# Splitting a unit's row maxima on GpSimd before they are transposed, in a fused attention and Fourier kernel

## The chip, the cores and the metric

The kernel runs on one core of one Trainium2 chip. The metric is the device time of one execution in microseconds; less is better. Times "before" are those of the kernel as it stood ahead of the change.

## The reference

Two sublayers read the same input, and a gate mixes them. Cut to what is computed:

```python
x = A_x                                           # (1, 2048, 640) float32
g = sigmoid((x * gate_w).sum(-1, keepdims=True))
# attention, 32 heads of width 20
qkv = (x @ wqkv).reshape(B, S, 3, 32, 20)         # q, k, v
p = softmax(q @ k.T * 20 ** -0.5)                 # per head, 2048 x 2048
a = (p @ v).reshape(B, S, 640) @ wo
# Fourier mixing of the same x
u, w = x @ dft_hid_re.T, x @ dft_hid_im.T
b = dft_seq_re @ u - dft_seq_im @ w
return g * a + (1 - g) * b
```

The weights wqkv and wo are drawn small and then multiplied by 64. The softmax subtracts each row's maximum.

## The kernel before

Most products are made from two rounded parts of each fp32 value (`split`: a rounded copy, then the rest as a second rounded value), by three matmuls (`three`). `R` is the rounded type (`float32r`), `F32` is plain fp32.

**Units.** The 32 heads are taken in 16 pairs; a pair's queries come in two halves of 1024. One pair with one half is a unit, so there are 32 units (`NU`). The stacks `qst` and `kst` hold, for each of the pair's two heads, 60 rows of split queries and keys in one half of the partitions (0 to 59 and 64 to 123). Behind them come two more rows: in `kst` ones, in `qst` the negated row maximum of each query, as a rounded part and its rest. So the second score matmul gives logits with the maximum subtracted already, and the exponential can follow at once.

**Two score passes.** In the first pass (`s_mm`, line 170) a step computes two 128 x 512 blocks of scores, and VectorE takes the maximum over 512 keys (`mx`, line 172). A unit has 32 such steps. When the last one is done, `max_nm` reduces the four partial maxima of each query and negates them (`nm`, 128 x 16, line 186), and `max_chain` transposes them on TensorE (line 204), splits the result on VectorE (lines 114 and 115 by way of `split`), and sends the rows into `qst` by four transfers on the SyncE queue (lines 212 and 213). In the second pass (line 873) scores are computed again, transposed and with the maximum in them; ScalarE takes the exponential (line 875). The av matmuls (line 532) multiply it by the values, with a column of ones for the sums. At a unit's end `unit_end` divides by the sums, which takes a way over DRAM and one multiplication on GpSimd (line 562).

**The order of work.** It is written out by hand. A head phase loads and projects; the last projections (`qk_tile`, lines 118 to 120) are mixed with `HEAD` segments. A segment is one tile of the Fourier transform along the hidden axis (line 362) with four steps of the first pass, and one comes with every third projection tile. Then comes the main loop of 256 cycles. A cycle follows the string `ORDER`: eight matmuls of the second pass ("e", four steps), eight of the first pass ("m"), filling matmuls ("F"), and at its end a burst ("B") with the av matmuls of two key blocks. The first pass is `LEAD` steps ahead of the second, so the last `LEAD` steps of the loop have no "m". The fillings are, in this order: the other tiles of the hidden transform (one for each cycle), 56 tiles of the transform along the sequence (three cycles each, `dft_step`, line 613), and 30 half rows of the output projection (line 684; one cycle each, the last `SLOW` ones two cycles).

**GpSimd and the transfers.** The transform along the sequence is made by seven products of sums of blocks (`PRODUCTS`). GpSimd adds the loaded blocks and splits them: cosine blocks into `part` (`load_c`: lines 493, 114, 115), two for each tile, made ahead through a ring of three buffers; and the other operand into `x` (`load_a`: lines 507, 114, 115) for the product that follows. It also adds finished tiles to earlier ones (`yt`, line 711). ScalarE and VectorE read a finished tile first (`m`, lines 632 and 633). Each engine takes its instructions in the order in which the program gives them out. `at_step(i, fn)` gives out a piece of work when the second pass comes to step i.

In `burst`, units whose maxima have just ended stand in the list `ends`: `max_nm` is given out first, `max_chain` after the av matmuls of the same burst.

Of the kernel before, what the change touches and what calls it, by code (L numbers as in the profile page):

```python
# [10 lines left out]
F32 = mybir.dt.float32  # L11
R = mybir.dt.float32r
AF = mybir.ActivationFunctionType
ALU = mybir.AluOpType
AX = mybir.AxisListType
# [3 lines left out]
P = 128  # L19
# [10 lines left out]
NU = 2 * NP  # L30
# [6 lines left out]
FIRST = {"e": (0, 0, 1, 1), "m": (1, 1, 1, 1)}  # L37


LEAD = 41  # L40


FILL = {4: (0, 8, 7, 0)}
HEAD = 10

# [12 lines left out]

LONG = (0, 0, 0, 0, 0, 0, 0)
FULL = 1
SLOW = 4
PRE = range(FULL, NS)
UNITS = len(PRODUCTS) * HT

# [3 lines left out]
def f32(ap):  # L70
    return ap.bitcast(F32)
# [3 lines left out]
def mix_kernel(ctx: ExitStack, tc: tile.TileContext, xa, wqk, wb, cdft, wo, out):  # L75
    nc = tc.nc
    pe, act, dve, pool, sp = nc.tensor, nc.scalar, nc.vector, nc.gpsimd, nc.sync
    ctx.enter_context(tc.manual_schedule())

    def pools(**kw):  # L80
        return ctx.enter_context(tc.tile_pool(**kw))

    const = pools(name="const", bufs=1)
    small = pools(name="small", bufs=1)
# [13 lines left out]

    ident = const.tile([P, P], F32, name="ident")
    make_identity(nc, ident)  # L100
    kst = [const.tile([P, S], R, name=f"kst{i}") for i in range(2)]
    qst = [const.tile([P, S], R, name=f"qst{i}") for i in range(2)]
    for t in kst:
# [6 lines left out]
    def split(dst1, dst2, src, e1, e2):  # L110
        if e1 is act:
            act.activation(dst1, src, AF.Copy)  # L112
        else:
            e1.tensor_copy(dst1, src)  # L114
        e2.tensor_tensor(dst2, src, f32(dst1), op=ALU.subtract)  # L115
# [8 lines left out]
    def bank():  # L124
        return ps_w.tile([P, 512], F32, name=f"ps{next(turn) % 5}")
# [23 lines left out]
    def q_unit(n):  # L149
        u = n % 2 * (S // 2)  # L150
        return qst[n // 2 % 2][:, u : u + S // 2]

    mx, nms, ends = {}, {}, []
    now, later = [-1], {}

    def at_step(i, fn):
        later.setdefault(i, []).append(fn)
# [16 lines left out]
    def s_end(i):  # L174
        n, s = divmod(i, 32)
        if n < NU and s == 31:
            if now[0] < 0:
                max_nm(n)
            else:
                ends.append(n)  # L180
        if s == 1 and 0 < n <= NU and now[0] < 0:
            max_chain(n - 1)

    def max_nm(n):
        nms[n] = small.tile([P, 16], F32, name="nm", bufs=2)
        dve.tensor_reduce(nms[n], mx.pop(n).rearrange("p h q c -> p (h q) c"), axis=AX.X, op=ALU.max, negate=True)

    def s_step(i):
        for fn in [s_mm(i, h) for h in range(2)]:
# [10 lines left out]

    def max_chain(n):
        q = q_unit(n)
        pt = bank()[:16, :P]
        pe.transpose(pt, nms.pop(n), ident)
        m1 = small.tile([16, P], R, name="m1")
        m2 = small.tile([16, P], R, name="m2")
        split(m1, m2, pt, dve, dve)

        def rows():
            for h in range(2):  # L210
                b = 64 * h + KROWS
                sp.dma_start(f32(q[b : b + 1, :]), f32(m1[8 * h : 8 * h + 8, :]))
                sp.dma_start(f32(q[b + 1 : b + 2, :]), f32(m2[8 * h : 8 * h + 8, :]))

        if now[0] < 0:
            rows()
        else:
            at_step(now[0] + 2, rows)
# [49 lines left out]
    def load_wqk(c):  # L268
        raw = raw_tile()[:, : ND * P].rearrange("p (d c) -> p d c", d=ND)
        sp.dma_start(raw, wqk[c])  # L270

        def finish():
            w = part_tile().rearrange("p z c -> p (z c)")[:, : 2 * ND * P].rearrange("p (z d c) -> p z d c", z=2, d=ND)
            split(w[:, 0], w[:, 1], raw, act, dve)
            wt[c] = w

        return finish
# [19 lines left out]
    def flush(keep=0):  # L297
        while len(stores) > keep:
            sp.dma_start(*stores.pop(0))
# [52 lines left out]
    def hid_tile(i, read_out):  # L352
        j, st = divmod(i, NS)
        hf, ri = divmod(j, 2)
        new_y(0), new_y(1)
        w = wt["b", 2 + j]
        t, cs = st // 4, slice(st % 4 * P, (st % 4 + 1) * P)
        for d in range(ND):
            for z, (xz, wz) in enumerate(((0, 0), (0, 1), (1, 0))):
                for h in range(2):  # L360
                    r = slice(64 * h, 64 * h + 64)
                    pe.matmul(yp[h][:, :HE], xs[xz][t][r, d, cs], w[r, wz, d, :HE],  # L362
                              start=d == 0 and z == 0, stop=d == ND - 1 and z == 2)
                if (d, z) != (ND - 1, 2):
                    yield
        a = raw_tile()[:, :HE]
        y0, y1 = yp[0][:, :HE], yp[1][:, :HE]

        def read():
            act.activation(a, y0, AF.Copy, scale=-1.0 if ri else 1.0)  # L370
            dve.tensor_tensor(a, a, y1, op=ALU.subtract if ri else ALU.add)  # L371

        read_out(read, (a_scr[ri, hf, st], a))
        yield


    def segment(i, steps):
        def read_out(read, args):
            read()
            stores.append(args)  # L380

        tile_ = hid_tile(i, read_out)
        for n in FILL[steps]:
            run_s(step + 1)
            for _ in range(n):
                next(tile_)
# [3 lines left out]
    def run_s(upto):  # L390
        nonlocal step
        while step < upto:
            s_step(step)
            step += 1
# [42 lines left out]
    for n, c in enumerate(order):  # L437
        for t in range(4):
            m = 4 * n + t
            if m % 3 == 0 and hid_done < HEAD:  # L440
                segment(hid_done, 4)
# [4 lines left out]
            if t == 1:  # L446
                if n + 1 < len(order):
                    fin()
                if n + 2 < len(order):
                    fin = load_wqk(order[n + 2])  # L450
    run_s(LEAD)
    flush()
# [219 lines left out]
    def out_tile(tt, hf):  # L672
        new_y(0), new_y(1)
        if hf == 0:
            k = tt - PRE[0]
            yo[tt] = f32(a_tile(1, 12 + k) if k < 4 else a_tile(0, k)).rearrange("p z c -> p (z c)")
            assert all(st[tt, h] == 0 for h in range(2))
            sp.dma_start(yo[tt], y_scr[tt])
        o = opre[tt]
        for d in range(ND - 1):  # L680
            for z, (oz, wz) in enumerate(((0, 0), (0, 1), (1, 0))):
                for h in range(2):
                    r = slice(64 * h, 64 * h + 64)
                    pe.matmul(yp[h][:, :HE], o[r, oz, d], wos[d, hf][r, wz], start=d == 0 and z == 0, stop=d == ND - 2 and z == 2)  # L684
                if (d, z) != (ND - 2, 2):
                    yield
        m = apool[0].tile([P, HE], F32, name="m", bufs=2)
        y0, y1 = yp[0][:, :HE], yp[1][:, :HE]
        g = gate[:, tt : tt + 1]

        def read():
            if now[0] < total - LEAD:
                act.activation(m, y0, AF.Copy, scale=g)
            else:
                dve.tensor_scalar(m, y0, g, 1.0, op0=ALU.mult, op1=ALU.mult)
            dve.scalar_tensor_tensor(m, y1, g, m, op0=ALU.mult, op1=ALU.add)

        def add():
            y = yo[tt][:, hf * HE : (hf + 1) * HE]
            pool.tensor_scalar(y, y, ngate[:, tt : tt + 1], float(signs[tt, hf]), op0=ALU.mult, op1=ALU.mult)  # L700
            pool.tensor_tensor(y, y, m, op=ALU.add)

        extras.append((now[0], read))
        extras.append((now[0] + 3, add))
        yield
# [35 lines left out]
    def start_dft():  # L741
        flush()
        wide.release()
        apool.append(pools(name="apool", bufs=1))
        make_sel()
# [25 lines left out]
    def read_later(read, args):  # L771
        extras.append((now[0], read))
        at_step(now[0] + 2, functools.partial(sp.dma_start, *args))

    HID = 4 * NS - HEAD
    fills = itertools.chain(*(hid_tile(HEAD + g, read_later) for g in range(HID)), itertools.chain.from_iterable(dft_step(g) for g in range(NS * UNITS)),
                            itertools.chain.from_iterable(out_tile(tt, hf) for tt in PRE for hf in range(2)))
# [3 lines left out]
    start = 4 * HID  # L781
# [10 lines left out]
    for u in range(2 * len(PRE)):  # L792
        n = 2 if u >= 2 * len(PRE) - SLOW else 1
        cycles.append((at_tile, at_tile + n, 3 * (ND - 1)))
# [42 lines left out]
    def end(i):  # L837
        if i % 4 == 2:
            c = i // 4
            if c + HEAD in (NS, 2 * NS):  # L840
                at_step(i + 2, load_wb(3 + (c + HEAD) // NS, pool, pool))
            if c in (HID - 18, HID - 17, HID - 16):
# [9 lines left out]

    heads = {"e": 0, "m": 2 * LEAD}

    def score(kind):
        x = heads[kind]
        heads[kind] += 1
        i, z = divmod(x, 2)
        h = z ^ FIRST[kind][(i - (LEAD if kind == "m" else 0) - 1) % 4]
        if kind == "m":  # L860
# [6 lines left out]
        if i < total:  # L867
# [8 lines left out]
            if z:  # L876
                end(i)

    def burst(c):
        for n in ends:  # L880
            max_nm(n)
        run_extras(max(done - HIDS, 0) // 3, 2)
        for kt in (2 * c, 2 * c + 1):
            av_step(now[0], kt // NS, kt % NS)
        while ends:
            max_chain(ends.pop(0))
        if c == HID - 1:
            start_dft()

# [139 lines left out]
```

## Time and profile before

| | |
|---|---|
| three runs before | 1882.94, 1883.07, 1885.08 us (median 1883.07) |
| profiled execution | 1884.04 us, its span 1882.3 us |
| granted TensorE clock | 1.00 |
| busy: PE, VectorE (DVE), ScalarE (ACT), GpSimd (POOL) | 1872.6, 1448.1, 1220.9, 1070.4 us |
| transposes of the maxima (line 204) | 32, 277 ns each |
| moved by transfers | 280.51 MB, mean 149 GB/s |

PE stands for the matmuls and PEld for the loads of weights. A row of a timeline gives the start in us, the duration in us, the engine, the line, the operation, what it writes and reads, shapes and count, and in brackets how long the engine was idle before it and what released it. A row of the groups gives, behind the bar, the busy time in us, the mean in ns of one, then the idle time before them in us and what ended most of it. A row of a stretch gives its length, then busy time and instructions of PE, PEld, DVE, ACT and POOL, the clock, the share of the transfer engines and GB/s. The end of a matmul is modelled, so matmul records can overlap.

### The profile page before, as it was taken

What the parts mean: (1) busy time and instruction counts of PE and PEld (TensorE: products, weight loads), DVE (VectorE), ACT (ScalarE), POOL (GpSimd) and SP (SyncE); (2) the same over time, 40 slices, a digit from 0 to 9 for tenths busy, and PEclk for the clock granted to TensorE, in tenths of its full rate; (3) what the DMA queues carried; (4) which work ended last, traced back from release to release, by engine and by line L of the source; (5) the groups of instructions that cost most, each with busy time, mean ns of one, the idle gap of its engine ahead of it and who ended that gap; (6) DMA issues with size and microseconds to landing.
All of it is one profiled execution on the core that took longest, in us unless ns stands there. A gap on an engine that the chain in (4) does not pass through costs nothing. (4 is left out here: it accounts for less than half of the span.)

```text
span 1882.3 us, 44545 instructions
## 1 busy us (share of the span) xinstructions
PE 1872.6 (99%) x17453; PEld 1357.0 (72%) x17453; DVE 1448.1 (77%) x2410; ACT 1220.9 (65%) x2353; POOL 1070.4 (57%) x936
## 2 busy tenths in 40 slices
PE   9999999999999999999999999999999999999998
PEld 8988777777776777767677776777767676766666
DVE  4143468989898888888888888888888888889954
ACT  4221147777777766767676676766767676677785
POOL 1234421010045896566899899778789988634433
PEclk9999999999999999999999999999999999999999
DMA  7843341212425473537666576546475747342214
GB/s 232 179 136 137 137 142 48 78 60 64 117 69 182 148 230 127 162 123 186 196 186 223 173 248 190 167 130 189 159 233 196 221 144 197 117 116 63 62 44 151
DMA packets 174597, 280.51 MB, mean 149 GB/s; under 512 B 44095, under 2 KB 106687, under 8 KB 174387
## 3 DMA queue, kind: packets, MB, share of 16 engines
q1 hardware_dynamic: 173427, 275.69, 48.2%
q0 software_dynamic: 960, 1.97, 0.6%
q8 instruction: 137, 2.24, 0.5%
q14 instruction: 73, 0.60, 0.1%
HBM read 213.37 MB, written 63.52 MB: 147 GB/s over the span
## 5 line engine op out<-in xcount | busy, mean ns | idle before, releaser
L172 DVE TENSOR_REDUCE mx<-ps 128x1 f32<-128x512 f32 x2048 | 1295.5, 684 | 219.4 <-PE ps L170 201.7
L875 ACT ACTIVATE p<-ps 128x512 f32<-128x512 f32 x2048 | 1087.6, 599 | 430.1 <-PE ps L170 230.3
L170 PE MATMUL ps<-kst,qst 60*128 60x512 f32 x2048 | 775.7, 413 | 1.5 <-DVE mx L172 1.4
L873 PE MATMUL ps<-qst,kst 62*128 62x512 f32 x2048 | 703.9, 414 | 0.1
L613 PE MATMUL yp<-x,part 64*128 64x320 f32 x5376 | 644.9, 307 | 0.0
L613 PEld LDWEIGHTS yp<-x,part 64*128 64x128 f32 x5376 | 579.3, 186 | 7.5
L532 PE MATMUL av<-p,v 128*21 128x512 f32 x4096 | 492.1, 596 | 0.0
L873 PEld LDWEIGHTS ps<-qst,kst 62*128 62x128 f32 x2048 | 337.0, 184 | 201.0 <-DVE mx L172 182.2
L170 PEld LDWEIGHTS ps<-kst,qst 60*128 60x128 f32 x2048 | 368.2, 184 | 15.0 <-issue 3.8
L115 POOL TENSOR_TENSOR part<-raw,part 128x1024 fp32r<-128x1024 f32 (+1 forms) x129 | 290.6, 2252 | 10.3
L532 PEld LDWEIGHTS av<-p,v 128*21 128x21 f32 x4096 | 98.4, 100 | 227.0 <-issue 224.8
L362 PE MATMUL yp<-wb,x 64*128 64x320 f32 x1920 | 227.6, 307 | 0.3 <-ACT raw L370 0.2
L114 POOL CAST part<-raw 128x1024 fp32r<-128x1024 f32 (+1 forms) x129 | 127.3, 987 | 166.7 <-PE yp L613 145.3
L362 PEld LDWEIGHTS yp<-wb,x 64*128 64x128 f32 x1920 | 202.1, 186 | 5.1 <-DVE raw L371 0.7
L493 POOL TENSOR_TENSOR raw<-raw,raw 128x1024 f32<-128x1024 f32 x77 | 185.1, 2404 | 26.6 <-DMA raw<-in_cdft 26.3
L562 POOL TENSOR_TENSOR o<-o,rb 128x512 f32<-128x512 f32 x31 | 40.1, 1294 | 149.5 <-DMA rb<-r_scr 105.1
L684 PE MATMUL yp<-x,part 64*128 64x320 f32 x720 | 96.0, 310 | 0.0
L118 PE MATMUL ps<-x,part 128*128 128x512 f32 (+1 forms) x236 | 91.2, 386 | 0.3
L120 PE MATMUL ps<-x,part 128*128 128x512 f32 (+1 forms) x236 | 89.7, 380 | 0.0
L119 PE MATMUL ps<-x,part 128*128 128x512 f32 (+1 forms) x236 | 89.4, 379 | 0.0
L115 POOL TENSOR_TENSOR x<-araw,x 128x320 fp32r<-128x320 f32 x96 | 83.9, 874 | 7.7
L684 PEld LDWEIGHTS yp<-x,part 64*128 64x128 f32 x720 | 81.7, 186 | 2.9
(85 smaller groups left out, 1079.6 us busy)
## 6 DMA issues: line engine op xcount, KB each, us to landing
raw<-in_cdft SPq DMA_DIRECT2D x192, 512.0 KB
araw<-a_scr SPq DMA_DIRECT2D x176, 160.0 KB
qk_scr<-p SPq DMA_DIRECT2D x40, 512.0 KB
kst<-qk_scr SPq DMA_DIRECT2D x90, 160.0 KB
qst<-qk_scr SPq DMA_DIRECT2D x90, 160.0 KB
a_scr<-raw SPq DMA_DIRECT2D x64, 160.0 KB
yt<-y_scr SPq DMA_DIRECT2D x64, 160.0 KB
y_scr<-yt SPq DMA_DIRECT2D x64, 160.0 KB
```

The costliest lines, as they stand in the source:

```text
L114: e1.tensor_copy(dst1, src)
L115: e2.tensor_tensor(dst2, src, f32(dst1), op=ALU.subtract)
L118: pe.matmul(ps, st1, mv1, start=first, stop=False)
L170: pe.matmul(ps, q[b : b + KROWS, qt * P : (qt + 1) * P], k[b : b + KROWS, kc * 512 : (kc + 1) * 512], start=True, stop=True)
L172: return lambda: dve.tensor_reduce(mx[n][:, h, qt, kc : kc + 1], ps, axis=AX.X, op=ALU.max)
L362: pe.matmul(yp[h][:, :HE], xs[xz][t][r, d, cs], w[r, wz, d, :HE], start=d == 0 and z == 0, stop=d == ND - 1 and z == 2)
L493: pool.tensor_tensor(raws[0], raws[0], raws[1], op=ALU.add if PRODUCTS[n][0][1][0] > 0 else ALU.subtract)
L532: pe.matmul(av[32 * j : 32 * j + DH + 1, :], v[:, kt, h * (DH + 1) : (h + 1) * (DH + 1)], pp[qc][:, h, :], start=kt == 0, stop=kt == NS - 1)
L613: pe.matmul(yp[h][:, :HE], c[r, cz, cs], a[r, az], start=s == 0 and z == 0, stop=s == NS - 1 and z == 2)
L684: pe.matmul(yp[h][:, :HE], o[r, oz, d], wos[d, hf][r, wz], start=d == 0 and z == 0, stop=d == ND - 2 and z == 2)
L873: pe.matmul(pt, k[b : b + KROWS + 2, kt * P : (kt + 1) * P], q[b : b + KROWS + 2, qc * 512 : (qc + 1) * 512], start=True, stop=True)
L875: act.activation(pts[n, kt, qc][:, h], pt, AF.Exp, scale=float(DH) ** -0.5)
```

## The change

The maxima are split before they are transposed. `max_nm` still reduces on VectorE, but then GpSimd splits the 16 columns into 32 rounded ones. `max_chain` turns these 32 columns by one matmul of the rounded type against a rounded identity (`turner`), VectorE copies the 32 x 128 result once, and two transfers, each with both parts of one head, take the place of four. In the main loop `max_chain` is called one burst later than `max_nm`, by way of the list `turned`; in the head eight steps later than before. `LEAD` goes from 41 to 45 steps, `HEAD` from 10 to 11 segments, `SLOW` from 4 to 5 half rows.

```diff
-LEAD = 41
+LEAD = 45
-HEAD = 10
+HEAD = 11
-SLOW = 4
+SLOW = 5
     make_identity(nc, ident)
+    turner = const.tile([P, P], R, name="turner")
+    pool.tensor_copy(turner, ident)
...
-        if s == 1 and 0 < n <= NU and now[0] < 0:
+        if s == 9 and 0 < n <= NU and now[0] < 0:
             max_chain(n - 1)

     def max_nm(n):
-        nms[n] = small.tile([P, 16], F32, name="nm", bufs=2)
-        dve.tensor_reduce(nms[n], mx.pop(n).rearrange("p h q c -> p (h q) c"), axis=AX.X, op=ALU.max, negate=True)
+        nm = small.tile([P, 2, 8], F32, name="nm", bufs=2)
+        dve.tensor_reduce(nm.rearrange("p h q -> p (h q)"), mx.pop(n).rearrange("p h q c -> p (h q) c"),
+                          axis=AX.X, op=ALU.max, negate=True)
+        nms[n] = small.tile([P, 2, 2, 8], R, name="nms", bufs=2)
+        split(nms[n][:, :, 0], nms[n][:, :, 1], nm, pool, pool)
...
     def max_chain(n):
         q = q_unit(n)
-        pt = bank()[:16, :P]
-        pe.transpose(pt, nms.pop(n), ident)
-        m1 = small.tile([16, P], R, name="m1")
-        m2 = small.tile([16, P], R, name="m2")
-        split(m1, m2, pt, dve, dve)
+        pt = bank()[:32, :P]
+        pe.matmul(pt, nms.pop(n).rearrange("p h z q -> p (h z q)"), turner, start=True, stop=True)
+        m = small.tile([32, P], F32, name="m12")
+        dve.tensor_copy(m, pt)

         def rows():
             for h in range(2):
                 b = 64 * h + KROWS
-                sp.dma_start(f32(q[b : b + 1, :]), f32(m1[8 * h : 8 * h + 8, :]))
-                sp.dma_start(f32(q[b + 1 : b + 2, :]), f32(m2[8 * h : 8 * h + 8, :]))
+                sp.dma_start(f32(q[b : b + 2, :]).rearrange("z (q c) -> z q c", c=P), m[16 * h : 16 * h + 16, :])
...
+    turned = []
+
     def burst(c):
         for n in ends:
             max_nm(n)
         run_extras(max(done - HIDS, 0) // 3, 2)
         for kt in (2 * c, 2 * c + 1):
             av_step(now[0], kt // NS, kt % NS)
-        while ends:
-            max_chain(ends.pop(0))
+        for n in turned:
+            max_chain(n)
+        turned[:] = ends
+        ends.clear()
```

## The prediction, made before the changed kernel ran

> **What bounds the kernel now.** I read the page first, for the span and the busy engines.
>
> ```profile
> span 1882.3 us, 44545 instructions
> ...
> PE 1872.6 (99%) x17453; PEld 1357.0 (72%) x17453; DVE 1448.1 (77%) x2410; ACT 1220.9 (65%) x2353; POOL 1070.4 (57%) x936
> ```
>
> TensorE (PE) is in work for all but 10 us; no other engine is over 77%. Matmul records overlap, so "99%" doesn't say that PE streams all the time. It says that a change pays only where it shortens the order of work on PE, and costs wherever PE is made to wait. So I read the timeline of PE next, around one burst (the av matmuls that close each cycle) that ends a unit's maxima, and around the burst after it.
>
> ```profile
> 1002.61 1.92 PE L532 MATMUL av<-p,v 128*21 128x512 f32 x16
> 1004.45 0.09 PEld L204 LDWEIGHTS ps<-ident,nm 128*16 128x16 f32 x1 [0.85 <-DVE nm L186]
> 1004.45 0.28 PE L204 MATMUL ps<-ident,nm 128*16 128x128 f32 x1
> 1004.66 0.18 PEld L873 LDWEIGHTS ps<-qst,kst 62*128 62x128 f32 x1
> ...
> 1009.12 1.91 PE L532 MATMUL av<-p,v 128*21 128x512 f32 x16
> 1010.97 0.18 PEld L873 LDWEIGHTS ps<-qst,kst 62*128 62x128 f32 x1 [0.85 <-DVE mx L172]
> ```
>
> In the ordinary burst the next weights load 1.85 us after av began (1009.12 to 1010.97). In the unit's burst the transpose's weights load 1.84 us after (1002.61 to 1004.45), and the scores follow 0.21 us later. So the 0.85 us that the view puts down to the maxima is no wait for them: it is there without a transpose too, put down to something else. The transpose costs PE 0.21 us a unit, 32 x 0.21 = 6.7 us in all, and that is the whole prize.
>
> **Part 1, the lead (LEAD, HEAD, SLOW).** The turn (the transpose, now a matmul against turner) comes one burst after the maxima; four steps more of lead keep it where it was against the exponentials. For that, one hidden-DFT segment with its four steps of maxima goes into the head, one cycle leaves the front of the main loop, and one half-filled cycle comes in at its end. PE's timeline of the last segment in the head, then of two bursts at the front and two at the end:
>
> ```profile
> 235.17 0.73 PE L170 MATMUL ps<-kst,qst 60*128 60x512 f32 x4
> ...
> 238.19 0.40 PE L170 MATMUL ps<-kst,qst 60*128 60x512 f32 x2
> 238.52 0.50 PE L118 MATMUL ps<-x,part 128*128 128x512 f32 x1
> ...
> 239.32 0.39 PE L118 MATMUL ps<-x,part 128*128 128x512 f32 x1
> 239.55 0.39 PE L119 MATMUL ps<-x,part 128*128 128x512 f32 x1
> ...
> 262.71 1.92 PE L532 MATMUL av<-p,v 128*21 128x512 f32 x16
> 268.94 0.63 PE L532 MATMUL av<-p,v 128*21 128x512 f32 x4
> ...
> 1827.38 2.08 PE L532 MATMUL av<-p,v 128*21 128x512 f32 x16
> 1832.04 2.08 PE L532 MATMUL av<-p,v 128*21 128x512 f32 x16
> ```
>
> A segment takes PE from 235.17 to 238.52, matmul after matmul: +3.35 us. The cycle that goes is worth 268.94 - 262.71 = 6.23, the one that comes 1832.04 - 1827.38 = 4.66: -1.57 us. Together +1.8 us. A segment holds the work that the lost cycle held beyond its exponentials and av, but in the main loop the maxima's matmuls run beside the exponentials' in the other half of the array, and in the head they don't. The first unit's rows are now turned in that last segment; the two projection tiles behind it, 30 matmuls at the 0.23 us between 239.32 and 239.55, leave 6.9 us until the first exponential: 0.
>
> **Part 2, the turn on PE.** It loads 32 columns for 16 and streams 128 columns of rounded type for 128 of fp32.
>
> ```profile
> L532 PEld LDWEIGHTS av<-p,v 128*21 128x21 f32 x4096 | 98.4, 100 | 227.0 <-issue 224.8 <-ACT p L875 1.7
> L118 PEld LDWEIGHTS ps<-x,part 128*128 128x128 f32 x236 | 44.4, 188 | 13.4 <-DVE mx L172 2.8 <-POOL x L701 0.8 <-ACT part L112 0.5
> L115 DVE TENSOR_TENSOR m<-ps,m 16x128 fp32r<-16x128 f32 x32 | 8.9, 278 | 1.1
> L204 PEld LDWEIGHTS ps<-ident,nm 128*16 128x16 f32 x32 | 2.8, 87 | 26.7 <-DVE nm L186 25.4 <-DVE m L696 0.8 <-ACT p L319 0.5
> ```
>
> Loads: 87 ns for 16 columns, 188 for 128, so about 101 for 32. Stream: of today's 0.21 us, 0.087 is the load and 0.12 the stream. No rounded matmul under 320 columns is in the trace. From below: the 512-column ones in the head follow each other by 0.23 us (239.32 to 239.55), a quarter of that is 0.058, the turn 0.16 and the gain 0.05 x 32 = 1.6 us. From above: a quarter of the columns takes as long as the 512, 0.23, the turn 0.33 and the loss 0.12 x 32 = 3.9 us. I take the stream as it is today, 0.12, because the nearest row is the transpose itself, of the same 128 columns: the load alone then counts, 0.014 x 32 = +0.4 us. The Trainium skill (TensorE: Matmul & The Clock Gate, Back-to-back issue gap) gives N/2.4 + 2.5 ns a matmul, an estimate of 56 ns here, and by it the term would be the lower end, -1.6; no run here shows it at 128 columns.
>
> VectorE loses one of three operations on PSUM (278 ns a unit). PE's next scores don't wait for it in the rows above: 0. SP issues two row transfers for four, and it already stands waiting for them:
>
> ```profile
> SPq L212 <- DVE m L115: 211.6, 31, 11.2
> ```
>
> So fewer of them shorten nothing, and as the turn keeps its place against the exponentials, the rows come no later: 0.
>
> **Part 3, the wait on GpSimd (POOL).** The negated maxima (nm) are now split by two POOL operations, queued in the burst ahead of everything that burst and later steps give POOL. POOL runs far ahead of PE; now it can't pass this point before VectorE has done nm. Behind it stand the loads' sums and splits: x (L507, L114, L115), the cosine blocks' part (L493, L114, L115), and yt. PE waits for part. The views are the page's groups, the timelines of POOL, DVE and ACT, and one stretch.
>
> ```profile
> L753 POOL COPY sel<-ident 128x32 f32<-128x32 f32 x4 | 0.7, 211 | 1.1 <-PE ps L170 1.1
> ```
> ```profile
> 945.76 0.88 POOL L507 TENSOR_TENSOR araw<-araw 128x320 f32<-128x320 f32 x1
> 952.87 0.20 DVE L186 TENSOR_REDUCE nm<-mx 128x16 f32<-128x64 f32 x1
> 1032.53 2.39 POOL L115 TENSOR_TENSOR part<-raw,part 128x1024 fp32r<-128x1024 f32 x1
> 1035.43 0.45 ACT L632 ACTIVATE m<-yp 128x320 f32<-128x320 f32 x1
> 1054.34 0.45 ACT L632 ACTIVATE m<-yp 128x320 f32<-128x320 f32 x1
> 1100.40 0.88 POOL L507 TENSOR_TENSOR araw<-araw 128x320 f32<-128x320 f32 x1
> 1105.08 0.21 DVE L186 TENSOR_REDUCE nm<-mx 128x16 f32<-128x64 f32 x1
> 1187.44 0.45 ACT L632 ACTIVATE m<-yp 128x320 f32<-128x320 f32 x1
> 1190.57 2.39 POOL L115 TENSOR_TENSOR part<-raw,part 128x1024 fp32r<-128x1024 f32 x1
> 1206.61 0.44 ACT L632 ACTIVATE m<-yp 128x320 f32<-128x320 f32 x1
> ```
> ```profile
> 1110.00:1212.00 102.00, 102.00 (x1032) 72.26 (x1029) 86.06 (x143) 71.20 (x136) 93.61 (x79) 1.00 0.64 194
> ```
>
> The two operations cost about 0.45 us a unit (two of 211 ns, the smallest copy). Nothing is late for the turn itself, a burst of 6.3 us later. What counts is what stands behind. The L507 rows are the operations that, by the new order, follow the split in two units: POOL began them at 945.76 and 1100.40, and nm was done at 953.07 and 1105.29. So POOL falls back 7.3 + 0.45 = 7.8 us there, and 4.9 + 0.45 = 5.3 us here. Over most of the run it makes that up in its idle time. In stretches such as 1110 to 1212 it can't: 93.61 of 102 us busy, and the other 8.4 us spread over 79 instructions, 0.1 us each, while both the running product and the next have two-term operands. There POOL lives on its lead. How much there is: an L632 copy marks the end of a tile; the second part of a tile is wanted half-way between two of them. Half-way between 1187.44 and 1206.61 is 1197.0, and POOL was done with that part at 1192.96: a lead of 4.1 us, the least that I found. POOL arrives 5.3 late from 1105, and 0.45 more from the next unit's split: 5.8 - 4.1 = 1.7 us, in which PE waits. In the product before, the wanted time is half-way between 1035.43 and 1054.34, 1044.9; done was 1034.92, a lead of 10.0 against 7.8 + 0.45: 1.8 us to spare, no loss. A third such stretch follows later; I take it as this second one. So +1.7 us; from below 0, as POOL gets only work and a wait, no relief; from above 7.5, if the other two had the lead of 4.1 as well (1.7 + 8.2 - 4.1 + 1.7).
>
> **The sum.** +1.8 (lead) + 0.4 (turn) + 1.7 (POOL) = +3.9 us. The profiled execution took 1884.04 us, 1.74 outside its span; with 3.9 it would be 1887.9. It lies 0.97 over the median of the three runs, 1883.07, so a median goes to 1887.0. A measurement of this kernel tells about 0.2%, 3.8 us, from no change: faster is under 1879.3, slower over 1886.8. The forecast is just over the edge.
>
> **The rivals.** (a) POOL's lead is enough and the turn streams at full rate: 1.8 - 1.6 = +0.2, 1883.3; some tenths more or 1.7 us of POOL, up to 1885. For: the lost time is a difference of two near numbers. Against: nothing in the trace shows 128 columns at full rate. (b) The turn's load goes under av. Its operand is ready 6 us before, and today's is not. Then only 0.058 of 0.21 stays, a gain of 0.15 x 32 = 4.9; with POOL at 0 the kernel is faster, 1883.07 + 1.8 - 4.9 = 1880.0. It decides from the point where the L204 load begins clearly less than 1.84 us after av. Against: the scores' load in the ordinary burst begins at 1.85 as well. The Trainium skill (TensorE: Matmul & The Clock Gate, Step-by-step: what each phase is for) has PE pull weight loads ahead of running matmuls when row groups don't conflict or the load goes to the background weights; the trace agrees among the scores, but not behind av, where both loads wait 0.85 us. (c) The turn streams four times slower a column: 1883.07 + 1.8 + 3.9 + 1.7 = 1890.5. For: fp32's 128 columns take 0.12 us, double the rounded rate, so short streams aren't known to be cheap. (d) All three stretches lose: 1887.0 + 5.8 = 1892.8. Against: the lead of 10.0 us above.
>
> **How the numbers follow.** The forecast's case has 0.35, of which I put 0.24 over the edge and 0.11 under; (a) 0.20, (b) 0.15, (c) 0.18, (d) 0.10, 0.02 for what I don't see. Slower: 0.24 + 0.18 + 0.10 = 0.52. Same: 0.11 + 0.20 + half of (b) 0.08 = 0.39. Faster: the rest, 0.09. The range 1882.5 to 1892 leaves out most of (b) below and the upper part of (d) above, under 2 in 10. Its cases of both signs lie close; the likeliest one's own range is 1885 to 1889.
>
> **What would show it.** The last segment of the head: eleven, each 3.35 us, the first av some 3.4 us later. The turn: load at av + 1.84, the scores 0.16, 0.22 or 0.33 after it. POOL: holes before the first split operation of 5 to 8 us, and in 1110 to 1212 one wait of PE for part of about 2 us, or none. I am wrong if the unit's burst costs PE nothing, if PE waits for part in more than one stretch, or if a wait for a unit's rows shows before its first exponential.

## The result and the profile after

| | before | after |
|---|---|---|
| median of seven runs (lowest to highest) | 1883.23 us (1882.71 to 1885.11) | 1890.51 us (1888.38 to 1891.53) |
| profiled execution, its span | 1884.04, 1882.3 us | 1890.83, 1889.0 us |

After to before is 1.0034, with a 95% interval of 1.0024 to 1.0044: slower, as the forecast of 1887.0 said, but by 7.3 us at the medians instead of 3.9. The time lies inside the range of 1882.5 to 1892, but above the 1885 to 1889 given for the likeliest case.

The page of the kernel after, the rows that answer to those shown of before (its lines stand two or three further down: the split is L116 and L117, the scores L172 and L876, av L535, the turn L209):

```profile
span 1889.0 us, 44474 instructions
...
PE 1875.3 (99%) x17453; PEld 1359.1 (72%) x17453; DVE 1442.8 (76%) x2378; ACT 1220.7 (65%) x2353; POOL 1082.3 (57%) x1001
```

VectorE has 5.3 us less work and GpSimd 11.9 us more. Neither explains 6.7 us of span, so I went to the timeline of PE and its weight loads: the first av, then an ordinary unit's end.

```profile
265.90 1.92 PE L535 MATMUL av<-p,v 128*21 128x512 f32 x16
272.14 1.91 PE L535 MATMUL av<-p,v 128*21 128x512 f32 x16
...
1056.55 1.92 PE L535 MATMUL av<-p,v 128*21 128x512 f32 x16
1058.39 0.11 PEld L209 LDWEIGHTS ps<-turner,nms 128*32 128x32 f32 x1 [0.85 <-issue]
1058.57 0.18 PEld L876 LDWEIGHTS ps<-qst,kst 62*128 62x128 f32 x1
```

The first av comes 3.19 us later (262.71 before). The turn loads 1.84 us after av, as the transpose did, and the scores follow 0.18 us behind it, where it was 0.21. So an ordinary unit's end got no dearer. The next view is the waits of the same kernel (total in us, times, longest), those that belong to the split:

```profile
POOL nms L116 <- DVE nm L188: 334.3, 26, 40.2
...
PEld ps L209 <- POOL nms L117: 5.7, 3, 3.1
...
PE ps L209 <- POOL nms L117: 2.9, 3, 2.2
```

GpSimd stands still 334 us in all in front of the split, which is mostly idle time moved there: GpSimd is 57% busy in both kernels. But in three units PE waits for the split itself, a wait that the prediction had ruled out. Where the worst one comes from is in GpSimd's timeline, at unit 17 and then at unit 18, one unit of 51 us later:

```profile
1095.35 0.87 POOL L117 TENSOR_TENSOR x<-araw,x 128x320 fp32r<-128x320 f32 x1
1102.34 0.20 POOL L116 CAST nms<-nm 128x16 fp32r<-128x16 f32 x1 [6.13 <-DVE nm L188]
...
1155.51 2.43 POOL L496 TENSOR_TENSOR raw<-raw,raw 128x1024 f32<-128x1024 f32 x1
1158.00 1.04 POOL L116 CAST part<-raw 128x1024 fp32r<-128x1024 f32 x1
1159.12 2.34 POOL L117 TENSOR_TENSOR part<-raw,part 128x1024 fp32r<-128x1024 f32 x1
1161.41 0.20 POOL L116 CAST nms<-nm 128x16 fp32r<-128x16 f32 x1
1161.68 0.22 POOL L117 TENSOR_TENSOR nms<-nm,nms 128x16 fp32r<-128x16 f32 x1
```

and in that of PE and its loads:

```profile
1157.87 1.91 PE L535 MATMUL av<-p,v 128*21 128x512 f32 x16
1161.95 0.11 PEld L209 LDWEIGHTS ps<-turner,nms 128*32 128x32 f32 x1 [3.09 <-POOL nms L117]
1161.96 0.25 PE L209 MATMUL ps<-turner,nms 128*32 128x128 f32 x1 [2.18 <-POOL nms L117]
```

At unit 17 GpSimd is early and stops for 6.13 us until VectorE has the maxima. From there to unit 18 its timeline shows no other wait. At unit 18 the split's turn in the queue comes behind a cosine block's sum and split (2.43 + 1.04 + 2.34 us); it ends at 1161.9, where PE wanted it at 1157.87 + 1.84 = 1159.7. PE's load waits 3.09 us instead of 0.85, that is 2.24 more. The cycle, from av to av, took 10.27 us where a unit's end takes 6.50, though: 3.78 more. The rest is in the windows of the same kernel, after the pause (length; PE, PEld, DVE, ACT, POOL busy; clock; transfers' share; GB/s):

```profile
1158.00:1163.00 5.00, 2.82 (x26) 1.14 (x20) 1.69 (x4) 1.33 (x3) 4.84 (x6) 1.00 0.73 239
1163.00:1164.00 1.00, 1.00 (x14) 1.00 (x12) 0.99 (x2) 0.81 (x2) 1.00 (x2) 0.77 0.04 13
1164.00:1166.00 2.00, 2.00 (x16) 2.00 (x15) 1.34 (x2) 1.39 (x3) 1.85 (x4) 0.50 0.24 60
1166.00:1167.50 1.50, 1.50 (x15) 1.50 (x14) 0.84 (x3) 0.91 (x2) 1.36 (x3) 0.68 0.45 122
```

After the pause PE was granted 0.77, 0.50 and 0.68 of its clock, in the mean of the last three windows (4.5 us together). Of those, 1.00 x 0.23 + 2.00 x 0.50 + 1.50 x 0.32 = 1.7 us are lost, which covers the 1.5 that the wait leaves over. Such a fall doesn't follow every pause of about this length (last section), so this part belongs to the profiled execution.

The two other waits for the split cost 0.3 and 0.5 us, so the split cost 4.6. The remainder of the 6.7 us: head and front +3.2, about -1.6 for the cycle exchanged, -1.0 for the turns (32 x 0.03), and +1.3 behind the last av. The head's part is that of two executions: with eleven segments the first av stands at 264.25 to 266.03 in nine profiles, with ten at 260.61 and 262.71. The last part is one slow issue of a transfer, in the chain that ended last (after, then before):

```profile
1871.39 1.90 SPq L971
```
```profile
1865.91 0.73 SPq L964
```

Nothing of the change leads to it: the same issue takes 1.91 us in the kernel below that has neither the split nor the long lead, and 0.72 to 0.74 in most of those that have one of them.

### The profile page after: what moved, and what is told of

It is laid out like the page before. It is cut to its first block, busy times and chain, and to the rows that moved or that the text cites. A ratio compares the mean times of both kernels' runs of the same rounds, so it can differ in the third digit from the quotient of the medians.

```text
span 1889.0 us, 44474 instructions
## 1 busy us (share of the span) xinstructions
PE 1875.3 (99%) x17453; PEld 1359.1 (72%) x17453; DVE 1442.8 (76%) x2378; ACT 1220.7 (65%) x2353; POOL 1082.3 (57%) x1001
## 3 DMA queue, kind: packets, MB, share of 16 engines
q8 instruction: 137, 2.24, 0.5%
## 5 line engine op out<-in xcount | busy, mean ns | idle before, releaser
L172 PE MATMUL ps<-kst,qst 60*128 60x512 f32 x2048 | 775.7, 414 | 1.6 <-DVE mx L174 1.4
L876 PE MATMUL ps<-qst,kst 62*128 62x512 f32 x2048 | 704.7, 415 | 0.1
L535 PE MATMUL av<-p,v 128*21 128x512 f32 x4096 | 492.5, 596 | 0.0
L876 PEld LDWEIGHTS ps<-qst,kst 62*128 62x128 f32 x2048 | 337.3, 185 | 200.6 <-DVE mx L174 155.9
L172 PEld LDWEIGHTS ps<-kst,qst 60*128 60x128 f32 x2048 | 368.1, 185 | 15.9 <-issue 4.7
L117 POOL TENSOR_TENSOR part<-raw,part 128x1024 fp32r<-128x1024 f32 (+1 forms) x129 | 290.2, 2250 | 10.3
L535 PEld LDWEIGHTS av<-p,v 128*21 128x21 f32 x4096 | 98.6, 100 | 227.1 <-issue 224.2
L116 POOL CAST nms<-nm 128x16 fp32r<-128x16 f32 x32 | 6.3, 197 | 334.3 <-DVE nm L188 334.3
L116 POOL CAST part<-raw 128x1024 fp32r<-128x1024 f32 (+1 forms) x129 | 127.1, 985 | 89.1 <-PE yp L616 72.0
L117 POOL TENSOR_TENSOR x<-araw,x 128x320 fp32r<-128x320 f32 x96 | 83.7, 872 | 7.7
```

What stands on the lines that cost most here:

```text
L172: pe.matmul(ps, q[b : b + KROWS, qt * P : (qt + 1) * P], k[b : b + KROWS, kc * 512 : (kc + 1) * 512], start=True, stop=True)
L535: pe.matmul(av[32 * j : 32 * j + DH + 1, :], v[:, kt, h * (DH + 1) : (h + 1) * (DH + 1)], pp[qc][:, h, :], start=kt == 0, stop=kt == NS - 1)
L876: pe.matmul(pt, k[b : b + KROWS + 2, kt * P : (kt + 1) * P], q[b : b + KROWS + 2, qc * 512 : (qc + 1) * 512], start=True, stop=True)
```

## The experiments

My theory: GpSimd's place in the order costs, because one hold is paid back a unit later with interest (a late turn and a lowered clock). Rivals: the longer lead costs it all; the turn's 32 rounded columns cost it on PE; or SyncE's transfers do. Each kernel was timed in five rounds beside the kernel before, whose median was 1882.69 for the first four kernels, 1882.89 for the next four and 1882.88 for the last two. Times given against before are differences of these medians.

**The lead alone** (kernel before):

```diff
-LEAD = 41
+LEAD = 45
-HEAD = 10
+HEAD = 11
-SLOW = 4
+SLOW = 5
```

> The kernel before with the three numbers alone changed (lead 45, eleven segments, five slow half rows); split and transpose as before. By the sum: +1.8 us over before (3.35 for the segment, -1.57 for the cycle), 1885.0, with no wait of PE for GpSimd. Rival, that the move of work into the head carries most of the loss: +5 us or more, 1888 and over.

1883.74 us (1882.88 to 1886.27), ratio 1.0006 (0.9997 to 1.0015): +1.05 us. The interval has both no loss and the forecast's 1.8 in it. So the lead isn't the 7.3 us.

**The split on VectorE** (kernel after):

```diff
-        split(nms[n][:, :, 0], nms[n][:, :, 1], nm, pool, pool)
+        split(nms[n][:, :, 0], nms[n][:, :, 1], nm, dve, dve)
```

> The changed kernel, but the two operations of the split run on VectorE; the turn stays one burst later. If GpSimd's place in the order makes the loss that stands beyond the lead: the waits of the turn go (in the changed kernel's profile three cycles are 3.8, 0.3 and 0.5 us longer), 4.6 us less than the changed kernel, 1884.5 to 1886. Rival, that VectorE pays: 32 times two small operations on an engine that is busy in the bursts, 0.4 us each on the path, +10 us.

1902.39 us (1900.97 to 1907.41), ratio 1.0109 (1.0096 to 1.0123): +19.7 us over before, 12.4 more than the change. My theory missed; the rival has the size, but not its way: it isn't 0.4 us at each unit, six cycles lose 1.8 to 3.4 us each. GpSimd no longer holds, but VectorE does. The groups of this kernel by shape, then its timeline at one unit's end:

```profile
L116 DVE CAST nms<-nm 128x16 fp32r<-128x16 f32 x32 | 20.8, 649 | 1.1
```
```profile
1055.25 2.35 POOL L117 TENSOR_TENSOR part<-raw,part 128x1024 fp32r<-128x1024 f32 x1
1055.56 2.07 DVE L116 CAST nms<-nm 128x16 fp32r<-128x16 f32 x1
1057.66 0.18 DVE L117 TENSOR_TENSOR nms<-nm,nms 128x16 fp32r<-128x16 f32 x1
...
1058.29 0.18 PEld L616 LDWEIGHTS yp<-x,part 64*128 64x128 f32 x1 [2.00 <-DVE m L636]
```

A copy of 16 columns takes 649 ns in the mean, and here 2.07 us: it began while a GpSimd operation ran and ended when that did (1055.25 + 2.35 = 1057.60). Behind it VectorE's copy of a finished tile is late, and PE waits for that. Half of the 32 copies of 16 columns take 0.18 us or less; the eleven that take over 0.5 us all end 0.02 to 0.05 us behind a GpSimd operation that ran when they began. The Trainium skill (SBUF — State Buffer, SBUF: two separate sides) has GpSimd and a VectorE operation in a two-port mode share one pair of ports, which whichever starts first keeps for its whole instruction while the other blocks; the trace agrees, with 2.07 us here, though no row shows the mode of this copy. So "off GpSimd" wasn't a clean undoing, and I undid one unit at a time.

**Unit 17's split on VectorE, the others on GpSimd** (kernel after):

```diff
-        split(nms[n][:, :, 0], nms[n][:, :, 1], nm, pool, pool)
+        e = dve if n == 17 else pool
+        split(nms[n][:, :, 0], nms[n][:, :, 1], nm, e, e)
```

> The changed kernel, but the split of unit 17 alone runs on VectorE. So GpSimd isn't held 6.1 us for unit 17's maxima, and unit 18's split is on GpSimd as before. If the hold one unit earlier makes the lateness: the wait of the turn of unit 18 goes, 3.8 us less than the changed kernel, and GpSimd ends that split over 2 us ahead of the turn. Rival, that GpSimd is late in that stretch anyway, by its load: the wait stays at 2 us or more, no change.

1885.98 us (1884.72 to 1892.33), ratio 1.0028 (1.0018 to 1.0038): +3.3 us. By the medians that is 4.0 us less than the change, but the intervals overlap; the profile tells more. This kernel's timeline at unit 18:

```profile
1155.19 0.20 POOL L116 CAST nms<-nm 128x16 fp32r<-128x16 f32 x1
...
1159.65 0.11 PEld L210 LDWEIGHTS ps<-turner,nms 128*32 128x32 f32 x1 [0.85 <-issue]
```

Unit 18's split comes at 1155.19 instead of 1161.41, 6.2 us earlier: the hold of 6.13 us at unit 17 made it late. Its cycle is back to 6.49 us, and the turn waits no longer than behind any av. But this execution lost 2.2 us elsewhere, at the first pass of a new pair. SyncE's row, then PE's:

```profile
990.16 0.36 SPq L829 DMA_DIRECT2D qst<-qk_scr  x1
...
997.63 0.47 PE L172 MATMUL ps<-kst,qst 60*128 60x512 f32 x1 [1.98 <-DMA y_scr<-yt]
```

The view puts this wait down to a store of yt, which the matmul doesn't read. What it does read was loaded by transfers of which the last was issued at 990.16, 7.5 us ahead of it. In the kernel before the same pair's last load was issued at 985 and its first matmul came at 1001, some 16 us later; the longer lead brought the first pass four steps nearer to its loads. I take that for the cause, but no run has shown it alone: with the long lead and the loads in their places this margin is 6.3 to 11 us, and PE waited there in the profiles of this kernel and the next only, not in the others, the kernel after (6.3 us) among them.

**Unit 18's split on VectorE, the others on GpSimd** (as above, `n == 18`):

> The changed kernel, but the split of unit 18 alone runs on VectorE: the turn can't wait for GpSimd there, the hold at unit 17 stays. If the lost lead is then missing further on, as in the prediction: PE waits for the cosine part some 35 us later, 1.5 to 2.5 us and the clock with it, so 1 to 2.5 us less than the changed kernel. Rival, that the lead for the part is enough: no wait at all, 3.8 us less.

1887.57 us (1886.23 to 1891.65), ratio 1.0028 (1.0016 to 1.0039): +4.9 us, by the medians 2.4 less than the change, with intervals that overlap. Unit 18's turn no longer waits, though GpSimd is as late as before. Now the loss that the prediction named appears where the prediction put it, in this kernel's timeline:

```profile
1196.24 0.70 PE L617 MATMUL yp<-x,part 64*128 64x320 f32 x6 [0.74 <-POOL part L117]
```

That cycle takes 7.54 us, 1.2 more than its neighbours. In the kernel after it doesn't show; there PE itself is 3.8 us later by then, more than those 1.2.

**No split at all, one rounded row, a burst later** (kernel after). VectorE's reduction writes the negated maximum rounded; the second part is left out, so the turn has 16 columns, one row a head is sent, and the second scores read one row fewer. A softmax doesn't change with the value that is subtracted, as long as numerator and sum use the same one.

```diff
...
-        nms[n] = small.tile([P, 2, 2, 8], R, name="nms", bufs=2)
-        split(nms[n][:, :, 0], nms[n][:, :, 1], nm, pool, pool)
+        nms[n] = small.tile([P, 16], R, name="nm", bufs=2)
+        dve.tensor_reduce(nms[n], mx.pop(n).rearrange("p h q c -> p (h q) c"), axis=AX.X, op=ALU.max, negate=True)
...
-            pe.matmul(pt, k[b : b + KROWS + 2, kt * P : (kt + 1) * P],
+            pe.matmul(pt, k[b : b + KROWS + 1, kt * P : (kt + 1) * P],
```

> The changed kernel with its lead of 45 and the turn a burst later, but without the split on GpSimd: rounded maxima from VectorE, one row a head, the second part left out. If the loss beyond the lead is GpSimd's hold: the kernel with the lead alone (1.05 us over before) less 1 us for the turn, so 1882 to 1884, and no wait of the turn. Rival, that the lag or the longer lead makes the loss: 1887 and over.

1884.37 us (1882.9 to 1887.31), ratio 1.0009 (1.0000 to 1.0018). With everything of the change kept but the split (and a row), 5.8 of the 7.3 us are gone, and the interval lies clear of that of the change. Some 0.6 of them is the narrower turn (32 x 0.02, next run).

**The same, in the same burst as the maxima, with the old lead** (also LEAD 41, HEAD 10, SLOW 4, and `max_chain` called as before the change):

> The turn alone: lead, segments and half rows as before, the turn in the burst of the maxima. VectorE writes the negated maxima rounded, they are turned by the rounded matmul, copied once, and one row a head goes into the stack; the second part of the maximum is left out, and the second scores read one row less. No GpSimd, no longer lead. In the changed kernel's profile the turn costs 0.18 us for 0.21: about -1 us against before, 1881.7. Rival, that the single pass needs the burst's delay, PE waiting for nm: over before.

1881.23 us (1880.01 to 1882.23), ratio 0.9989 (0.9981 to 0.9998): -1.7 us, faster than both kernels. Its loads at a unit's end:

```profile
1001.24 0.09 PEld L206 LDWEIGHTS ps<-turner,nm 128*16 128x16 f32 x1 [0.85 <-DVE nm L188]
1001.40 0.18 PEld L873 LDWEIGHTS ps<-qst,kst 61*128 61x128 f32 x1
```

The rounded turn costs PE 0.16 us a unit for 0.21: 32 x 0.05 = 1.6 us, the size of the gain. What one VectorE operation less and one row less add isn't shown apart.

**That kernel with the long lead** (LEAD 45, HEAD 11, SLOW 5; still in the same burst):

> The single rounded maximum with the rounded turn in the same burst (no GpSimd split), but with 45 steps of lead, eleven segments and five half rows. It stands between the kernel with 41 steps (1881.23) and the one that has 45 steps and turns a burst later (1884.37), and tells the two parts of their 3.1 us apart. If the lead alone costs what it cost by itself (1.05 us), 1882.3. If the later turn costs nothing and the lead all of it, 1884.4. My theory is the first with some tenths more, since the first passes of a new pair come 4 steps nearer to their loads: 1882.3 to 1883.3.

1883.81 us (1882.17 to 1886.97), ratio 1.0007 (0.9998 to 1.0016), above what I expected. So of the 3.1 us between the two kernels above, 2.6 come with the lead; the 0.5 left for the later turn lies within the noise. The profiled executions differ by 0.9 us only, 1882.17 against 1881.28, but that of the short lead is the one with the issue of 1.91 us at its end. Without it some 2.1 are left: the first av comes 3.9 later, and the loop is 1.7 shorter.

**That kernel with a shorter lead still** (LEAD 37, HEAD 9, SLOW 3):

> The turn alone as in the run with the old lead, but with a lead of 37 steps, nine segments and three slow half rows: the exchange of the prediction run the other way. A cycle of 6.23 comes in front, 3.35 and 4.66 go: -1.8 us against the turn alone by the sum, -1.05 by what the lead alone measured; 1880 to 1881. Rival, that the rows come too late: the first exponential of a unit stands 4.3 us after the turn for 10.6, the rows leave until 1.9 and take some 2 to land; where they miss, up to 1 us a unit, +10 us or more.

1883.4 us (1881.95 to 1884.87), ratio 1.0003 (0.9994 to 1.0011). That is 2.2 us over the kernel with the old lead, where I expected 1 or 2 less; the rival's +10 isn't there either. The head's 3.2 us are saved, but now the rows come late. PE waits for them three times, 1.9 us in all; the longest:

```profile
604.51 0.59 PE L873 MATMUL ps<-qst,kst 61*128 61x512 f32 x2 [1.33 <-DMA qst<-m]
```

**The loads of a new pair given out two a step** (kernel after), to give back the margin of the first pass:

```diff
-                    at_step(i + 2 + j, functools.partial(sp.dma_start, *args))
+                    at_step(i + 2 + j // 2, functools.partial(sp.dma_start, *args))
```

> The changed kernel, but the twelve loads of the next pair's stacks are given out two a step, so the last lies five steps earlier. In the profiles the last of them is issued 6 us ahead of the first maxima matmul of the pair, 14 before the change, and in two of the experiments PE stands there for 1 and 2 us. If that is a second loss that the longer lead brings: no such wait, 0.5 to 2 us less than the changed kernel and less spread. Rival, that the spread has another source, or the loads sent earlier delay others: no change or slower.

1896.46 us (1892.21 to 1903.95), ratio 1.008 (1.0066 to 1.0093): worse, against my expectation. GpSimd's timeline of this kernel:

```profile
1095.03 2.40 POOL L496 TENSOR_TENSOR raw<-raw,raw 128x1024 f32<-128x1024 f32 x1 [8.02 <-DMA raw<-in_cdft]
...
1163.86 0.20 POOL L116 CAST nms<-nm 128x16 fp32r<-128x16 f32 x1
```

GpSimd waited 8.02 us for a cosine block, whose transfers SyncE issued behind the crowded loads (from 1084.94; from 1075.89 in the kernel after), so unit 18's split came at 1163.86, 2.5 us later than in the kernel after, and its cycle took 12.27 us. The profiled execution was the fastest of its six; the 4 us more of the median I have not traced.

**The split given out two steps later in the main loop** (kernel after):

```diff
-        split(nms[n][:, :, 0], nms[n][:, :, 1], nm, pool, pool)
+        (at_step if now[0] >= 0 else lambda i, f: f())(now[0] + 2, lambda t=nms[n]: split(t[:, :, 0], t[:, :, 1], nm, pool, pool))
```

> The changed kernel, but in the main loop GpSimd's two split operations are given out two steps (half a cycle, some 3.1 us) later, behind the GpSimd work of those steps; their number, the turn and the lead stay. Theory (the place in GpSimd's queue costs, not the two operations): at unit 17 the split now stands behind an x sum with its split (2.2 us) and a part sum with its split (5.8 us) more, so GpSimd, which reached the old place 6.13 us early, doesn't stop there at all; the split of unit 18 stands behind a yt and an x more (3.9 us), and from the 1155.19 that it had without the hold it comes at about 1159.1 to 1159.6, where PE wants it at 1159.65. The cycle of 10.27 us goes back to about 6.5, the holds before the split's first operation, 334 us in all, shrink to under half, and the median is 1884 to 1887. Rival (the split is late wherever it stands, and each later place makes it later): unit 18's turn waits 2 us or more again, with more units beside it, and the median is 1890 or more.

1887.46 us (1884.34 to 1890.05), ratio 1.0023 (1.0014 to 1.0032): +4.6 us. Its GpSimd timeline at unit 17 and unit 18, then PE's:

```profile
1101.82 2.40 POOL L117 TENSOR_TENSOR part<-raw,part 128x1024 fp32r<-128x1024 f32 x1
1104.17 0.19 POOL L116 CAST nms<-nm 128x16 fp32r<-128x16 f32 x1
...
1158.90 0.20 POOL L116 CAST nms<-nm 128x16 fp32r<-128x16 f32 x1
```
```profile
1156.09 1.91 PE L535 MATMUL av<-p,v 128*21 128x512 f32 x16
1159.45 0.25 PE L209 MATMUL ps<-turner,nms 128*32 128x128 f32 x1 [1.45 <-POOL nms L117]
```

The same operations at another place: no hold at unit 17, and unit 18's split at 1158.90, just ahead of the expected 1159.1 to 1159.6. But PE ran ahead of the kernel from which I had taken 1159.65: its av began at 1156.09, so it wanted the split at 1157.9, and it stood for 1.45 us; the cycle took 8.01 instead of 10.27 us. The holds fell from 334 to 256 us, not under half. Against before, the loss fell by 2.7 us, a little short of what I expected, and the intervals overlap; the traces show the mechanism more surely than the times do.

## Why the prediction was right or wrong

**Direction: right, and for the reasons given, the lead and GpSimd.** GpSimd, held at the split, loses the lead on which it lives from 1110 to 1212. The amount, 7.3 for 3.9 us, was short mostly by the GpSimd term.

**The lead (+1.8): the step holds.** In the profile it is 3.2 - 1.6 = 1.6. Alone it measured +1.05 us, in an interval that has 1.8 in it; on the faster kernel +2.6. One thing was missing from that step: the loads of a new pair's stacks stay where they are in the order while the first pass that reads them comes four steps earlier. That margin, 16 us before, was 7.5 in an execution that lost 2 us there.

**The turn (+0.4, bounds -1.6 to 3.9): wrong nearest row.** I took the stream of the fp32 transpose, 0.12 us, for the rounded one. Measured, 0.18 us in all, of which the load is 0.106: 0.07 for the stream, near the lower bound's 0.058. The term is -1.0. The row of the same size was the wrong neighbour; that of the same type was the right one. The estimate of 56 ns by the Trainium skill's formula (TensorE: Matmul & The Clock Gate, Back-to-back issue gap) was nearer than my choice.

**GpSimd (+1.7): the mechanism was right; "nothing is late for the turn itself, a burst of 6.3 us later" failed.** The step compared when the maxima are ready with when the turn wants them, as if the split ran at once. In its queue it stands behind 5.8 us of a cosine block, and that work was itself late by the 6.1 us of the hold. The term is 4.6 us: 2.2 of the wait, 1.5 of lowered clock, 0.8 in two other units. By the medians the split costs some 5.2 (5.8 less the narrower turn). The forecast's own arithmetic (late by 5.8, lead of 4.1) pointed to the right place for `part`: with unit 18's turn no longer waiting, PE stood for it at 1196.24, 0.74 us, and the cycle lost 1.2 for the 1.7 forecast.

**Vector work, rows and SyncE (0): right.** In the kernel after PE waits for no unit's rows. They came late only with a lead of 37 steps.

The sum by the measured terms is 3.2 - 1.6 - 1.0 + 4.6 + 1.3 = 6.5 us against 6.7 of span. That it closes so well is in part luck: the profile before has a cycle of 7.16 us (at 576.66) where that after has 6.2, which the sum leaves out, and smaller differences make up for it. Rival (c) has the right time, 1890.5, by a mechanism that isn't there: the turn didn't stream slower. Rival (b) is out too: the turn loads 1.84 us after av, though its operand was ready long before. Of rival (a), the turn's rate came true and GpSimd's sufficient lead didn't; (d) is out, since in the kernel after PE waits for `part` in no stretch.

## What to carry to other kernels

An operation moved to an engine that runs ahead can cost its place in that engine's queue, not its 0.2 us. Work out both sides: what is held behind it when the engine arrives early, and what stands ahead of it when the engine arrives late, since one hold can make the other. If an edit changes by how many steps two streams are apart, list every transfer that is timed by the one and read by the other. And ask first whether the moved work is needed: dropping the second part of the maximum did more than any place for it.

## What the runs showed of the hardware that I had not expected

**A short pause can lower PE's clock, and its length alone doesn't decide.** Pauses of PE of 1.45 us (the split given out later) and 1.98 us (unit 17's split on VectorE) left it at 1.00; one of 2.18 us (kernel after) and one of 4.22 us (loads two a step) brought 0.50 for some microseconds. The windows after the pauses of 1.45, 1.98 and 4.22:

```profile
1161.00:1163.00 2.00, 2.00 (x26) 1.99 (x25) 1.95 (x4) 1.88 (x5) 2.00 (x2) 1.00 0.34 123
```
```profile
997.60:999.00 1.40, 1.37 (x16) 1.40 (x18) 0.86 (x2) 0.00 (x0) 1.26 (x3) 1.00 0.83 240
```
```profile
1164.40:1166.00 1.60, 1.59 (x11) 1.38 (x13) 1.12 (x3) 0.82 (x2) 1.60 (x3) 0.69 0.11 40
1166.00:1168.00 2.00, 2.00 (x17) 1.91 (x16) 1.19 (x2) 1.01 (x3) 1.85 (x4) 0.50 0.10 20
```

The kernel with every split on VectorE has six pauses of 1.59 to 1.67 us. After two of them the clock fell to 0.50, after the other four it stayed at 1.00. One of each kind, with a window that follows:

```profile
1058.30 0.41 PE L616 MATMUL yp<-x,part 64*128 64x320 f32 x1 [1.65 <-DVE m L636]
1060.00:1062.00 2.00, 2.00 (x17) 2.00 (x15) 1.38 (x2) 1.30 (x3) 1.54 (x1) 0.50 0.00 0
```
```profile
1524.99 0.41 PE L616 MATMUL yp<-x,part 64*128 64x320 f32 x1 [1.67 <-DVE m L636]
1526.00:1528.00 2.00, 2.00 (x26) 2.00 (x24) 1.84 (x4) 1.86 (x5) 2.00 (x1) 1.00 0.00 0
```

The price was about 1.5 us after either of the long pauses: the cycles of 10.27 and 12.27 us, less 6.50 for a usual one and less what the load waited over 0.85 us (2.24, and 5.14 - 0.85 = 4.29). It was the same after the short ones: 9.87 us for the cycles with the fall, 8.28 to 8.35 for those without. The Trainium skill (TensorE: Matmul & The Clock Gate, What's actually happening) puts the fall at an idle window of about 3.4 us; here 1.65 us were enough. What decides beside the length, no run here shows.

**A copy of 16 columns from SBUF to SBUF on VectorE is no fixed price.** It took 0.18 us or less in half of the cases and 2.07 us in the row above, where it ended with a GpSimd operation; the mean was 649 ns. The same size on GpSimd itself took 197 ns in the kernel after.
